# Recurrent-memory attention and MLP: DMA bounces kept apart from DMA transposes, new orders of work, idle matmuls before WO, and W1 in two pieces

## The chip, the cores and the metric

The kernel runs on one core of one Trainium2 chip. The metric is the device time of one execution in microseconds (us); the time before is the median of 12 runs. Engines are called PE (TensorE matmul), PEld (TensorE weight load), DVE (VectorE), ACT (ScalarE), POOL (GpSimd) and SP (SyncE, which here only issues DMAs).

## The reference

The input x has 2048 tokens of 512 values in bfloat16. It is layer-normalised and cut into 64 segments of 32 tokens. An attention layer with 32 heads of 128 runs over the segments one after the other; 8 memory rows, which are the layer's own output of the segment before, stand ahead of each segment:

```python
for s in range(n_seg):                       # 64 segments, strictly one after the other
    h = concatenate([mem, xs])               # 8 memory rows + 32 tokens
    q, k, v = h @ Wq, h @ Wk, h @ Wv         # 512 -> 32 heads x 128
    p = softmax(where(mask, q k^T * scale, -1e9))
    o = (p v) @ Wo                           # 4096 -> 512
    mem = o[:8];  outs.append(o[8:])
h  = x + concatenate(outs)
h2 = h + gelu(layernorm(h) @ w1 + b1) @ w2 + b2    # 512 -> 1792 -> 512
```

## The kernel before

The kernel is recorded as a list of operations by the class Sched and then planned. Each operation has an engine, a duration that the planner believes, and the names that it reads and writes; the waits follow from these names. The planner places the operations of ACT, DVE, POOL and SP by rank (the longest chain behind an operation) plus a table BONUS; an operation recorded with `either` goes to the engine where it would end first. TensorE's order is not planned: it is written by hand in START (segment 0) and ORDER (four lists, one for each segment of a block of four, the position being called sg). BANKS says which PSUM bank a part uses, and BACK which passes run through their four column groups backwards, so that two neighbouring passes can share a loaded weight.

The tokens of a segment are split: 24 of them together with the 8 memory rows form the 32 rows of part A (hT), which depends on the segment before. The other 8 tokens of each of four segments together form the 32 rows of part B (hB), which depends on nothing but x. The parts in ORDER are these:

- Q0, Q1, K0, K1, V0, V1: the passes of part A, each a half of the heads, 16 matmuls of 512 columns on four 32-column tiles (one_pass).
- F0, F1: such passes of part B, for the next block; FB: the output projection of part B for the block before.
- SC0, SC1: scores of the 8 tokens of part B and the memory rows, followed by a softmax on DVE and ACT (sc_mm, sc_softmax); SA: scores of the 24 tokens (sa_mm).
- PV0, PV1, PVA: products with V (pv_c, pv_a); WO: the output projection in eight units (wo, wo_units), of which the 8 memory rows go through a transpose on DVE (TT) and two adds into hT, and so start the next segment.
- TR: DMA transposes. ln1 normalises a block of x and transposes it into hT, from where POOL copies part B's rows into hB. nat transposes a finished block of output (opT) into xT, adds it to x (xr) and stores it (h_mid).

The V of part B is needed in another layout. v_B_spread writes it from VSB to DRAM (v_last, four DMAs) and reads it back into VBD (four DMAs); the text calls this a bounce. On SP all DMAs stand in one queue in the planner's order. The loads at the start are chained in the order x, WV, WK, WQ, WO, more x, with at most three big pieces in flight. After the last segment, WK's space receives the MLP's W1 and W2.

The planner believes that any DMA lands 2 us after its issue (`HOP["sp"]`):

```python
    def lat(p, o):
        if p.is_dma:
            return HOP["sp"]
```

TensorE's program has about 44,000 instructions. `far` cuts it at one place in each 256 instructions, puts a compare-and-branch there (L338; it is never taken) and behind it a prefetch hint for the branch that follows (L342), whose other target lies two cuts on. LINE_AT is the place of the first instruction in its 256, LINE_HINT the place from which a cut may be made, LINE_FIRST that of the extra first hint.

Of the kernel before, what the change touches and what calls it, by code (L numbers as in the profile page):

```python
# [21 lines left out]
LINE_N, LINE_AT, LINE_HINT, LINE_FIRST = 256, 192, 168, 128  # L22
HALVES = ("kqP", "KA", "ZCm", "QA", "VS", "nmc", "EC", "rsc", "PC", "PTC", "OTm", "KB", "QTB", "VSB", "QT")
BONUS = {"EC0": -8.13, "KA0": 12.71, "KA1": -29.28, "KB0": 5.95, "KB1": 40, "OTB": -5.75, "OTm0": 4.47, "OTm1": -45.52, "OTx": 8.96,
         "PA": -27.46, "PC0": 14.2, "PC1": -1.38, "PTC0": -32.47, "PTC1": 12.99, "QT0": -6.56, "QT1": 3.35, "QTB0": 10.94, "QTB1": 14.21,
         "TT": -9.53, "VBD": 3.74, "VS0": 4.35, "VS1": -40, "VSB0": -4.69, "VSB1": 40, "ZCb": -40, "ZCm0": 3.61, "ZCm1": -4.02, "ag": 16.27,
         "hB": 0.6, "hd": -12.71, "hx": 2.32, "kqP0": -0.04, "kqP1": -4.86, "kqP2": -15.51, "kqP3": 14.67, "kqP4": -40, "kqP5": -4.52,
         "nma": -0.27, "nmc1": 22.51, "opB": -1.68, "ps": -16.05, "rs": 2.11, "rs2": 1.39, "rsa": -7.92, "rsc0": -9.47, "rsc1": 10.24,
         "sma": 6.14, "st": 4.36, "st2": -40, "vd": -0.77, "xT": -40, "xn": -3.59, "xn4": -40, "xr": -40}
LEAN = 10.341  # L30
# [4 lines left out]
          (("Q0", 0, 3), ("TR", 0, 1), ("Q0", 3, 4), ("K0", 0, 4), ("Q1", 0, 4), ("K1", 0, 4), ("SC0", 0, 1), ("V0", 0, 4), ("V1", 0, 2),  # L35
           ("SC1", 0, 1), ("V1", 2, 4), ("F0", 0, 1), ("PVA", 0, 1), ("PV0", 0, 1), ("F0", 1, 3), ("WO", 0, 3), ("PV1", 0, 1),
           ("F0", 3, 4), ("WO", 3, 8), ("F1", 0, 1), ("SA", 0, 1), ("F1", 1, 4)),
          (("Q0", 0, 2), ("Q1", 0, 1), ("Q0", 2, 3), ("TR", 0, 1), ("Q0", 3, 4), ("K0", 0, 4), ("Q1", 1, 4), ("K1", 0, 4), ("SC0", 0, 1),
           ("V0", 0, 4), ("V1", 0, 2), ("SC1", 0, 1), ("F0", 0, 2), ("V1", 2, 3), ("PVA", 0, 1), ("PV0", 0, 1), ("V1", 3, 4), ("F0", 2, 4),
           ("WO", 0, 2), ("PV1", 0, 1), ("WO", 2, 8), ("SA", 0, 1), ("F1", 0, 4)),  # L40
          (("Q0", 0, 3), ("TR", 0, 1), ("Q0", 3, 4), ("K0", 0, 4), ("Q1", 0, 4), ("K1", 0, 4), ("SC0", 0, 1), ("V0", 0, 4), ("V1", 0, 1),
           ("PVA", 0, 1), ("SC1", 0, 1), ("F0", 0, 1), ("V1", 1, 4), ("PV0", 0, 1), ("F0", 1, 2), ("SA", 0, 1), ("WO", 0, 2),
           ("PV1", 0, 1), ("WO", 2, 8), ("F0", 2, 4), ("F1", 0, 4)),
          (("Q0", 0, 1), ("TR", 0, 1), ("Q0", 1, 2), ("K0", 0, 1), ("Q0", 2, 4), ("K0", 1, 4), ("Q1", 0, 4), ("K1", 0, 4), ("SC0", 0, 1),
           ("V0", 0, 4), ("V1", 0, 2), ("SC1", 0, 1), ("V1", 2, 4), ("FB", 0, 2), ("PV0", 0, 1), ("FB", 2, 4), ("WO", 0, 2), ("PVA", 0, 1),
           ("PV1", 0, 1), ("WO", 2, 8), ("FB", 4, 6), ("SA", 0, 1), ("FB", 6, 8)),
)
BANKS = (
    dict(Q0=4, Q1=4, K0=7, K1=5, V0=6, V1=5, SC0=7, SC1=4, F0=6, F1=5, FB=6, SA=7, WO=4),
    dict(Q0=6, Q1=4, K0=7, K1=5, V0=7, V1=5, SC0=6, SC1=4, F0=6, F1=5, FB=6, SA=7, WO=4),  # L50
    dict(Q0=6, Q1=4, K0=7, K1=5, V0=7, V1=5, SC0=6, SC1=4, F0=6, F1=5, FB=4, SA=7, WO=4),
    dict(Q0=6, Q1=4, K0=7, K1=5, V0=6, V1=5, SC0=7, SC1=4, F0=6, F1=5, FB=6, SA=7, WO=4),
)
BACK = (("Q1", "K0", "V0", "V1", "F0", "F1"), ("K0", "K1", "F1"), ("K0", "V1", "F0"), ("Q1", "K1"))
BANK0 = dict(K0=7, K1=5, Q0=4, Q1=7, V0=4, V1=5, SC0=6, SC1=7, F0=6, F1=4, FB=6, SA=4, WO=5)
START = (("B", "V", 0, (6, 7)), "V0", "V1", ("B", "K", 0, (4, 6)), "K0", "K1", ("B", "K", 1, (4, 6)), ("B", "Q", 0, (5, 6)), "Q0", "Q1", "Z",
         "SC0", "SC1", ("B", "Q", 1, (5, 4)), "PV0", "PV1", "SA", ("B", "V", 1, (6, 7)), "WO")


class Op:  # L60
    __slots__ = ("eng", "fn", "reads", "writes", "idx", "gidx", "deps", "sig", "sigcount", "waits",
                 "name", "is_dma", "dma_sem", "dur", "mode", "rank", "start", "succ", "prev", "ni", "dma_count", "alts", "kind",
                 "held", "loads", "seg")

    def __init__(self, eng, fn, reads, writes, name, dur, mode):
# [9 lines left out]
        self.alts = self.held = None  # L75
        self.loads = [4]
        k = writes[0] if writes else ""
# [3 lines left out]
class Sched:  # L81
# [60 lines left out]
    def dma(self, fn, kb, reads=(), writes=(), after=(), name=None, eng="sp", behind=None):  # L142

        line = self.dmas if eng == "sp" else self.soft
        old = line[-DMA_SEMS] if len(line) >= DMA_SEMS else None
        o = self.op(eng, fn, reads, writes, 0.07 + kb / 390.0 if eng == "sp" else 1.0, 0, name, list(after) + [old])
        o.is_dma = True
        o.prev = behind
        o.dma_count = 16 * (len(line) // DMA_SEMS + 1)
        line.append(o)  # L150
        return o
# [11 lines left out]
    def lat(p, o):  # L163
        if p.is_dma:
            return HOP["sp"]
        if p.eng == "pe" and o.eng == "pe":
            return 0.0
        return HOP[p.eng] + (0.02 if o.eng == "pe" else 0.0)
# [148 lines left out]
    def far(self, nc, e, zero):  # L317

        ops = self.streams["pe"]
        n, lines, cuts, early = 0, -1, [], None  # L320
        for i, o in enumerate(ops):
            line, at = divmod(n - LINE_AT, LINE_N)
            if early is None and line == 0 and at >= LINE_FIRST:
                early = i
                n += 1
            if line > lines and at >= (LINE_HINT if line else 200):
                assert at < 240
                cuts.append(i)
# [962 lines left out]
```

## Time and profile before

| | us |
|---|---|
| median of 12 runs | 847.77 |
| lowest, highest | 840.73, 852.89 |
| profiled execution, device time | 848.49 |
| its span, first to last instruction | 846.8 |
| PE busy / ACT / DVE / POOL | 791.3 / 583.8 / 520.6 / 179.8 |
| DMA xT<-opT, issue to landing, 14 times (lowest, median, highest) | 2.4, 3.9, 4.3 |
| DMA VBD<-v_last on SP, 56 times (median) | 5.5 |

The span has three stretches: the load of the weights until about 61 us, the 64 segments until about 728 us, and the MLP. A line such as "L667" is a line of the kernel before; passes have the line of a helper (L667, or L433 for matmuls that keep the loaded weight), so groups are told apart by their tiles, which are written out<-in. In the list of waits, "PE ... <- DVE hT" says that TensorE was idle until DVE had written hT; "issue" says that it was idle and that no semaphore explains it. A mean matmul duration in these tables includes the time in the array's pipeline, so the step from one group of four matmuls to the next (0.216 us for 512 columns) is shorter than the duration of one (0.38 us).

### The profile page before, as it was taken

The numbers are of one execution on the slowest core, as the hardware profiler recorded it, in microseconds if no ns is written. First come the engines' busy times: TensorE is split into PE (matmuls) and PEld (weight loads), VectorE is DVE, ScalarE is ACT, GpSimd is POOL, SyncE is SP. The second block draws the span as 40 slices with busy tenths as digits, with TensorE's granted clock in tenths as the row PEclk, the third lists the DMA queues.
The fourth block names the chain that finished last, engine by engine and source line by source line (L and its number), as shares of the span: only waits on it lengthen the run. The fifth ranks groups of instructions, "written<-read, shape, count | busy, mean of one in ns | idle before, by whom it ended". The sixth has DMA issues, their size and how long they took to land.

```text
span 846.8 us, 48411 instructions
## 1 busy us (share of the span) xinstructions
PE 791.3 (93%) x22173; PEld 433.1 (51%) x21613; DVE 520.6 (61%) x1637; ACT 583.8 (69%) x1579; POOL 179.8 (21%) x412
## 2 busy tenths in 40 slices
PE   1758999999899999999999899899999998999998
PEld 0234555555555555555555455455555554554443
DVE  3147667777586868686868576567676776632111
ACT  1337787878687878787878677678787877634442
POOL 3214112222121313131212121212121212042200
PEclk9879999999999999999999999999999999999999
DMA  8951002020202020202020202110111111511000
GB/s 337 367 181 36 9 12 41 16 38 21 41 11 42 17 41 17 41 16 42 16 42 20 44 11 34 16 29 17 29 17 29 41 29 17 196 45 50 25 26 25
DMA packets 49224, 44.15 MB, mean 52 GB/s; under 512 B 18164, under 2 KB 44668, under 8 KB 49020
## 3 DMA queue, kind: packets, MB, share of 16 engines
q1 hardware_dynamic: 48124, 40.00, 17.3%
q8 instruction: 173, 2.83, 1.4%
q0 software_dynamic: 896, 1.06, 0.5%
q14 instruction: 31, 0.25, 0.1%
HBM read 28.98 MB, written 8.39 MB: 44 GB/s over the span
## 4 chain that ended last, share of the span: by engine, by line
PE 84%; DMA 5%; ACT 5%; DVE 3%; issue 2%; SPq 0%; POOL 0%
PE ps L667 42%; PE ps L921 18%; PE ps L1181 6%; PE quad L1188 6%; PE ps L433 3%; PE quad L838 3%; DMA WQ<-in_A_Wq_dram 2%; PE ps L808 2%; PE quad L893 2%; PE ps L867 2%; ACT EC L820 1%; DMA WV<-in_A_Wv_dram 1%; ACT kqP L682 1%; ACT kqP L681 1%; DMA WK<-in_A_Wk_dram 1%
## 5 line engine op out<-in xcount | busy, mean ns | idle before, releaser
L921 PE MATMUL ps<-WO,OT 128*32 128x256 bf16 x4224 | 145.4, 279 | 4.3 <-issue 3.0
L667 PE MATMUL ps<-WQ,hT 128*32 128x512 bf16 x1920 | 130.9, 383 | 5.5 <-DVE hT L927 5.3
L667 PE MATMUL ps<-WV,hT 128*32 128x512 bf16 x1984 | 132.7, 382 | 0.1
L682 ACT ACTIVATE kqP<-ps 128x512 bf16<-128x512 f32 x160 | 95.0, 595 | 46.9 <-PE ps L667 43.8
L681 ACT CAST OT<-quad 128x128 bf16<-128x128 f32 (+1 forms) x192 | 85.0, 443 | 55.0 <-PE quad L842 49.2
L667 PE MATMUL ps<-WK,hT 128*32 128x512 bf16 x1736 | 119.0, 379 | 0.0
L921 PEld LDWEIGHTS ps<-WO,OT 128*32 128x32 bf16 x4224 | 100.4, 97 | 32.4 <-ACT OT L681 9.3
L681 ACT CAST kqP<-ps 128x512 bf16<-128x512 f32 x160 | 93.6, 585 | 21.3 <-PE ps L667 19.9
L709 DVE STREAM_TRANSPOSE KALL<-kqP 128x256 uint32<-128x256 uint32 x160 | 69.3, 433 | 51.0 <-ACT kqP L681 50.6
L679 POOL COPY ZC<-QT 128x128 bf16<-128x128 bf16 x127 | 38.0, 299 | 238.3 <-DVE QT L709 238.1
L667 PEld LDWEIGHTS ps<-WQ,hT 128*32 128x32 bf16 x1920 | 47.2, 97 | 72.2 <-issue 19.8
L667 PEld LDWEIGHTS ps<-WK,hT 128*32 128x32 bf16 x1736 | 47.9, 96 | 63.5 <-issue 26.5
L820 ACT ACTIVATE EC<-ps,nmc 128x64 f32<-128x64 f32 x256 | 77.9, 309 | 3.3 <-DVE nmc L816 2.5
L1184 ACT ACTIVATE WQ<-ps,b1t 128x512 bf16<-128x512 f32 x56 | 38.5, 687 | 58.4 <-PE ps L1181 58.0
L681 ACT CAST VS<-ps 128x512 bf16<-128x512 f32 x128 | 75.1, 587 | 2.2 <-PE ps L667 1.5
L709 DVE STREAM_TRANSPOSE QT<-kqP 128x256 uint32<-128x256 uint32 x128 | 55.3, 432 | 29.2 <-ACT kqP L682 27.6
L933 DVE STREAM_TRANSPOSE TT<-ps 128x256 f32<-128x256 f32 x66 | 29.7, 450 | 64.9 <-PE ps L921 63.8
L667 PEld LDWEIGHTS ps<-WV,hT 128*32 128x32 bf16 x1984 | 47.9, 96 | 31.1 <-ACT kqP L681 7.4
L1188 PE MATMUL quad<-WK,WQ 128*128 128x512 bf16 x224 | 54.4, 379 | 0.5 <-DVE xr L974 0.5
L879 ACT ACTIVATE SA<-SA 128x256 f32<-128x256 f32 x64 | 26.7, 417 | 37.6 <-DVE SA L878 33.8
L1232 DVE TENSOR_TENSOR WV<-quad,WV 128x512 bf16<-128x512 f32 x16 | 11.1, 691 | 66.0 <-PE quad L1188 66.0
L820 ACT ACTIVATION_READ_ACCUMULATOR EC<-ps,nmc 128x1 f32 x256 | 50.3, 197 | 0.0
(115 smaller groups left out, 1299.3 us busy)
## 6 DMA issues: line engine op xcount, KB each, us to landing
WV<-in_A_Wv_dram SPq DMA_DIRECT2D x4, 1024.0 KB, 6.0
WK<-in_A_Wk_dram SPq DMA_DIRECT2D x4, 1024.0 KB, 8.0
WQ<-in_A_Wq_dram SPq DMA_DIRECT2D x4, 1024.0 KB, 8.8
WO<-in_A_Wo_dram SPq DMA_DIRECT2D x4, 1024.0 KB
v_last<-VSB SPq DMA_DIRECT2D x56, 64.0 KB, 2.3
VBD<-v_last SPq DMA_DIRECT2D x56, 64.0 KB
WK<-in_B_w_dram SPq DMA_DIRECT2D x2, 1792.0 KB, 10.6
xr<-in_A_x_dram SPq DMA_DIRECT2D x16, 128.0 KB, 3.4
```

The costliest lines, as they stand in the source:

```text
L667: ins = e.matmul(o, l, m, start=start, stop=stop, tile_position=(0, 32 * j), skip_group_check=True)
L679: "pool": (lambda e: e.tensor_copy(out, src), 0.16 + 1.05e-3 * n)}
L681: return {"act": (lambda e: e.copy(out, src), t_act(n, ps_)), "dve": (lambda e: e.tensor_copy(out, src), 0.165 + 1.0e-3 * n * fast)}
L682: return {"act": (lambda e: e.mul(out, src, scale_), t_act(n, ps_)), "dve": (lambda e: e.tensor_scalar(out, src, scale_, None, ALU.mult), ...
L709: S.op("dve", lambda e: e.transpose(dst.bitcast(U32), kqP[:, i, :].bitcast(U32)), reads=[("kqP", i)], writes=[key], dur=0.435)
L820: ins = e.activation(EC[:, r, sl, :], ps[bank][:, 64 * sl:64 * sl + 64], ACTF.Exp, bias=nmc[:, r, sl:sl + 1], accum_out=smc[:, r, sl:sl + 1])
L879: S.op("act", lambda e: e.activation(SA[:], SA[:], ACTF.Exp), reads=["SA"], writes=["SA"], dur=t_act(256, False))
L921: ins = e.matmul(ps[bank][32 * j:32 * j + 32, 0:256], lhs(slot(h)), wo_cols(h, b), start=(k == 0), stop=(k == 15), tile_position=(0, 32 * ...
L933: S.op("dve", lambda e: e.transpose(tt.rearrange("p c q t -> p (c q t)"), ps[bank][:, 0:256]), reads=[("ps", bank)], writes=[("TT", par)], ...
L1181: ins = e.matmul(ps[bank][:, 0:SBT], W1[:, cc, fc * P:(fc + 1) * P], hnT_of(k, cc // 2)[:, cc % 2, :], start=(cc == 0), stop=(cc == DC - 1))
L1184: S.op("act", lambda e: e.activation(gT[:, fc, :], ps[bank][:, 0:SBT], ACTF.Gelu_apprx_tanh, bias=b1t[:, fc:fc + 1], scale=1.0), reads=[(" ...
L1188: S.op("pe", lambda e: e.matmul(quad[:, t, :], gT[:, fc, t * P:(t + 1) * P], W2[:, fc, :], start=(fc == 0), stop=(fc == FC - 1)), reads=[" ...
```

## The change

The change has these parts.

1. A name "turn" is added. Each DMA transpose (in ln1 and in nat) writes it; each bounce DMA reads it. So a transpose is issued only when all bounce DMAs recorded before it and the transpose before it have landed, and a bounce DMA only when the transpose before it has.
2. Each DMA has its own believed landing time (lag): 4.0 us for hT, 3.2 for xT, 3.2 for the bounce's writes, 5.0 for its reads, 2.0 for others.
3. The bounce of block 1 is issued by SP instead of POOL. nat's add into xr is fixed on DVE (before, the planner chose POOL).
4. stir: 12 matmuls into bank 7 that nothing reads, between units 3 and 4 of the first WO.
5. START is reordered: V of block 1 comes ahead of Q, and Q0 between the two halves of block 0's Q. ORDER, BANKS, BACK, BONUS and LEAN have new values. In ORDER K0 now leads a segment, and SA ends it.
6. far makes its first cut and its first hint one line of 256 earlier, and picks each cut among the places from 172 to 228 by the length of the matmuls around it, with a small weight on the later place.
7. W1 is loaded in two pieces, each with its own name; the MLP's W1 groups wait for their own half.

```diff
-LINE_N, LINE_AT, LINE_HINT, LINE_FIRST = 256, 192, 168, 128
+STIR = 12
+LINE_N, LINE_AT, LINE_HINT, LINE_LAST, LINE_FIRST, LINE_Q, LINE_W = 256, 192, 172, 228, 80, 24, 0.005
...
 ORDER = (
-          (("Q0", 0, 3), ("TR", 0, 1), ("Q0", 3, 4), ("K0", 0, 4), ("Q1", 0, 4), ("K1", 0, 4), ("SC0", 0, 1), ("V0", 0, 4), ("V1", 0, 2),
-           ("SC1", 0, 1), ("V1", 2, 4), ("F0", 0, 1), ("PVA", 0, 1), ("PV0", 0, 1), ("F0", 1, 3), ("WO", 0, 3), ("PV1", 0, 1),
-           ("F0", 3, 4), ("WO", 3, 8), ("F1", 0, 1), ("SA", 0, 1), ("F1", 1, 4)),
...
+          (("K0", 0, 4), ("Q0", 0, 4), ("Q1", 0, 4), ("K1", 0, 4), ("SC0", 0, 1), ("V0", 0, 1), ("TR", 0, 1), ("V0", 1, 4), ("V1", 0, 2),
+           ("SC1", 0, 1), ("F0", 0, 2), ("V1", 2, 3), ("PVA", 0, 1), ("PV0", 0, 1), ("V1", 3, 4), ("F0", 2, 4), ("WO", 0, 2),
+           ("PV1", 0, 1), ("WO", 2, 8), ("F1", 0, 4), ("SA", 0, 1)),
...
-START = (("B", "V", 0, (6, 7)), "V0", "V1", ("B", "K", 0, (4, 6)), "K0", "K1", ("B", "K", 1, (4, 6)), ("B", "Q", 0, (5, 6)), "Q0", "Q1", "Z",
-         "SC0", "SC1", ("B", "Q", 1, (5, 4)), "PV0", "PV1", "SA", ("B", "V", 1, (6, 7)), "WO")
+START = (("B", "V", 0, (6, 7)), "V0", "V1", ("B", "K", 0, (4, 6)), "K0", "K1", ("B", "K", 1, (4, 6)), ("B", "V", 1, (7, 5)),
+         ("B", "Q", 0, (4, None)), "Q0", ("B", "Q", 0, (None, 5)), "Q1", "Z", "SC0", "SC1", ("B", "Q", 1, (5, 7)), "PV0", "PV1", "SA", "WO")
...
         if p.is_dma:
-            return HOP["sp"]
+            return p.lag
...
-        n, lines, cuts, early = 0, -1, [], None
+        early, per, m = None, [], 0
+        for o in ops:
+            per += [o.dur / o.ni] * o.ni
+        n, lines, cuts, cand = 0, -2, [], []
         for i, o in enumerate(ops):
             line, at = divmod(n - LINE_AT, LINE_N)
-            if early is None and line == 0 and at >= LINE_FIRST:
+            if early is None and line == -1 and at >= LINE_FIRST:
                 early = i
                 n += 1
-            if line > lines and at >= (LINE_HINT if line else 200):
+                line, at = divmod(n - LINE_AT, LINE_N)
+            if cand and (line > cand[0][0] or at >= LINE_LAST):
+                cuts.append(max(cand, key=lambda c: c[1:])[-1])
+                lines = cand[0][0]
+                cand = []
+                n += 2
+                line, at = divmod(n - LINE_AT, LINE_N)
+            if line > lines and at >= LINE_HINT:
                 assert at < 240
-                cuts.append(i)
-                lines = line
-                n += 2
+                cand.append((line, min(sum(per[max(0, m - LINE_Q):m]), 0.4) + min(sum(per[m:m + LINE_Q]), 0.3) + at * LINE_W, i))
+            m += o.ni
             n += o.ni + (len(o.waits) >= 2)
+        cuts += [c[-1] for c in cand[-1:]]
...
-                      writes=[("hTx", tb % RBLK)] + [("hTm", r0 + k) for k in range(4)])
+                      writes=[("hTx", tb % RBLK)] + [("hTm", r0 + k) for k in range(4)] + ["turn"], lag=4.0)
...
-            eng = "pool" if bk < 2 else "sp"
+            eng = "pool" if bk < 1 else "sp"
...
+        def stir(n, bank):
+
+            def f(e):
+                return [e.matmul(ps[bank][:, :], ident[:], WV[:, 0, 0:512], start=True, stop=True) for k in range(n)][-1]
+            S.op("pe", f, reads=["ident", ("WV", 0, 0)], writes=[("ps", bank)], dur=0.2 * n, mode=MC, ni=2 * n)
...
             for q in range(8):
+                if idle and q == 4:
+                    stir(*idle)
...
-            S.either({"dve": (add, 0.45), "pool": (add, 1.15)}, reads=["xT", ("xr", bk % XR)], writes=[("xr", bk % XR)])
+            S.op("dve", add, reads=["xT", ("xr", bk % XR)], writes=[("xr", bk % XR)], dur=0.43)
...
-        S.dma(lambda e: e.dma_start(W1, w1_d), 1792, writes=["W1"], after=used["WK"])
+        for a_, b_ in ((0, F // 2), (F // 2, F)):
+            S.dma(lambda e, a_=a_, b_=b_: e.dma_start(W1[:, :, a_:b_], w1_d[:, :, a_:b_]), 896, writes=[("W1", a_ > 0)], after=used["WK"])
         S.dma(lambda e: e.dma_start(W2, w2_d), 1792, writes=["W2"], after=used["WK"])
```

The transpose in nat gets `"turn"` and `lag=3.2` in the same way; the bounce's writes get `reads=["turn"] + ...` with `lag=3.2`, its reads the same with `lag=5.0`.

## The prediction

> **What bounds the kernel now.** I read the busy time by stretches first, with cuts at the end of the weight loads (61 us) and at the end of the recurrence (728 us). Columns: stretch, its length, busy time and instructions of each engine, granted TensorE clock, DMA share, GB/s.
>
> ```profile
> 31.00:61.00 30.00, 14.94 (x292) 7.45 (x288) 7.91 (x24) 8.57 (x24) 7.22 (x14) 0.72 0.81 252
> 61.00:728.00 667.00, 648.63 (x20682) 363.97 (x20126) 475.89 (x1537) 514.93 (x1456) 142.63 (x336) 0.99 0.13 27
> ```
>
> From 61 to 728 us TensorE is busy 648.6 of 667 us: the recurrence is bound by TensorE, and only 18.4 us of idle time can be won there. From 31 to 61 us it is idle for half the time, at a clock of 0.72. Next the waits of TensorE (total, times, longest):
>
> ```profile
> PE quad L838 <- issue: 9.9, 4, 5.7
> PE ps L667 <- DMA WQ<-in_A_Wq_dram: 5.8, 3, 2.2
> PE ps L667 <- DVE hT L927: 5.3, 6, 1.4
> PE ps L921 <- issue: 3.0, 1, 3.0
> PE ps L667 <- issue: 2.5, 1, 2.5
> PE ps L1181 <- DMA WK<-in_B_w_dram: 1.3, 1, 1.3
> ```
>
> "issue" is idle time with no semaphore behind it: 15.4 us, the largest item after the prologue. The timeline of TensorE shows where it lies; nearly all is in four stalls: 5.73, 2.45, 3.54 and 3.03 us.
>
> ```profile
> 32.69 0.65 PE L667 MATMUL ps<-WQ,hB 128*32 128x512 bf16 x8 [1.62 <-DMA WQ<-in_A_Wq_dram]
> 35.34 1.04 PE L667 MATMUL ps<-WQ,hB 128*32 128x512 bf16 x8 [2.00 <-DMA WQ<-in_A_Wq_dram]
> 38.59 1.04 PE L667 MATMUL ps<-WQ,hB 128*32 128x512 bf16 x8 [2.20 <-DMA WQ<-in_A_Wq_dram]
> ...
> 53.27 0.19 PE L838 MATMUL quad<-PTC,VS 32*128 32x16 bf16 x1 [5.73 <-issue]
> ...
> 53.69 3.62 PE L667 MATMUL ps<-WV,hB 128*32 128x512 bf16 x32
> 57.06 2.73 PE L921 MATMUL ps<-WO,OT 128*32 128x256 bf16 x64
> 61.22 1.26 PE L667 MATMUL ps<-WQ,hT 128*32 128x512 bf16 x20 [1.43 <-DVE hT L927]
> ```
>
> The first stall ends at one PV matmul amid its group of 16, so no data was missing: the instruction itself was. The 32 WV matmuls after it take 3.62 us where the same pass takes 1.89 us elsewhere. The other three end at 228.05, 484.12 and 532.66 us. I looked at what the DMA queues do shortly before the first of them:
>
> ```profile
> 213.53 2.27 SPq L770 DMA_DIRECT2D VBD<-v_last  x4
> 215.90 1.22 SPq L624 DMA_TRANSPOSE hT<-xn  x1
> 226.41 1.19 SPq L954 DMA_TRANSPOSE xT<-opT  x1
> ```
>
> Four bounce reads are issued, and 0.1 us after them an hT transpose, while the reads take 5.5 us (median) to land. TensorE's prefetch hint (L342) of that moment stands at 215.65 us, and no instruction packet (queue q8) moves from then to 222.39 us. In the other two cases hT transposes at 471.19 and 519.34 us meet hints at 471.28 and 519.50 us, and again the next packet comes 6.7 and 7.6 us after the hint, against at most 4.8 us after any other hint of the recurrence past 56 us. So three hints, the only ones within 0.3 us of an hT transpose with bounce reads in flight, go unserved, and TensorE later runs into the line of code that never came. Two hints within 0.1 us of transposes with no bounce reads in flight (73.02 us), or with the last few packets of them (69.24 us), were served in 3.4 and 2.2 us.
>
> **What the Trainium skill says.** "Runtime: NRT & Kernel Launch", Instruction fetch mechanics: instruction memory is refilled in 16 KiB blocks of 256 instructions by a DMA queue of the sequencer's own. The page agrees: q8 moved 2.83 MB in 173 packets, 16 KB each. "DMA: Bandwidth & Descriptors", Rules for kernel authors: a transpose next to ordinary DMAs "needs nothing". That is about correctness; the three cases above say that it costs time here. "TensorE: Matmul & The Clock Gate", What's actually happening: after about 3.4 us idle the array runs at half rate until it was busy as long. The 3.62 us pass agrees.
>
> **The change part by part**, against the profiled execution: 848.49 us, span 846.8, 0.7 us above the median of twelve runs.
>
> *Start.* V of block 1 (32 matmuls) moves from behind SA to ahead of Q, and Q0 of segment 0 ahead of the second half of the block's Q. Until 30.47 us nothing changes. V then takes 32/4 x 0.216 = 1.73 us, to 32.2, inside the wait for WQ; the second WQ piece (32.69) lets half a block pass and Q0 run to 34.0; the fourth (38.59) lets the rest and Q1 run to about 40. Before, Q0 and Q1 ended at about 42.2 and PV1 began at 47.28, so 5.1 us later; now PV1 begins at about 45, and WO at about 46, if no stall intervenes. The early hint moves from 27.7 us to the masks (behind the second group of matmuls), and each following one stands a line of code earlier, so lines 1 to 3 are asked for before the WO traffic instead of in it: I take the 5.73 us stall as gone. What is late next is WO. The load stream runs at about 345 GB/s until 52 us, and its last 0.79 MB (six pieces of x and b2 behind WO) take 2.3 us of that: WO's last piece lands at about 49.7. WO units 0 to 3 take 0.94 us, to 47; the 12 idle matmuls 12 x 0.216 = 2.6 us, to 49.6, covered by WO's arrival; without that cover they cost 2.6. Units 4 to 7 end at 50.8; transpose 0.45, two halves of 0.20 and hand-overs let segment 1 begin at about 52.6 instead of 61.22. I take **8.4 us** (6 to 9.5), the stall included.
>
> *Bounces and transposes apart.* SP's order per block becomes four writes, four reads, xT transpose, hT transpose, h_mid, x load; before, hT came right behind the reads. Each transpose now waits for the reads, or the transpose before it, to land. On SP h_mid and the x load queue behind the later hT: about 10 us (from 215.90 to just behind 226.41). The hB copy on POOL waits for hT, with POOL busy 21%; hT is needed a block later. So the waits cost nothing: their cover is a block of 42 us. The three losses go: 2.45 + 3.54 + 3.03 = **9.0 us**. The spread of the runs, 840.73 to 852.89, fits some losses more or fewer; the lowest is 7.8 below the profiled one. New coincidences can't be excluded: 0 to 9 us back, I take 1. The bounce of block 1 moves from POOL to SP: eight issues of 0.52 to 0.69 us leave POOL, and on SP eight of 0.5 to 0.6 us stand behind WO's four, ahead of which nothing waits; the x loads behind four of them start some 2.4 us later, and x of block 2 may land near 53 us, just as DVE wants it (0 to 1 us, inside the start's range).
>
> *xr add from POOL to DVE.* 14 adds of 1159 ns leave POOL for about 0.42 us each on DVE (L974's row). In the built order each stands right behind PTC, and QTB's transpose, statistics and TT stand behind it. POOL waited 77.9 us for xT unharmed; DVE now waits if xT (2.4, median 3.9, at most 4.3 us from issue) comes after the 3.2 us planned. Bounds 0 and 14 x 0.7 = 9.8 us; most is filler work, I take 1.
>
> *W1 in two pieces.* SP issues W1a, W2, W1b. W1 landed 7.94 us after issue, so half of it in about 4, ahead of TensorE's 734.98: the **1.25 us** wait goes. W1b now lands last, near 728.6 + 13.5 = 742; its first reader is the eighth W1 group, at about 748. If that cover went, it would cost what it is late.
>
> *Order, banks, branches, planner.* In the built programs changes between 32-row, 32-column and full matmul groups go from 301 to 303, at about 0.12 us each: nothing. Kept weights go from 560 to 756 matmuls; in this trace four kept ones take 0.22 us like four others: nothing. K0 comes first and Q0 is followed by Q1 and K1 only. From Q0's end to the first score matmul lie ACT 0.595 + DVE 0.432 + POOL 0.299 + about 0.43 of hand-overs (read around 221 us) = 1.76 us, and the cover is 2 x 0.864 = 1.73: even, 0 to 0.4 us a segment. Gains from the other idle time: at most 18.4 - 9.0 us, I take none.
>
> Sum: -8.4 - 9.0 + 1 + 1 - 1.25 = -16.7, so 831.8; less the 0.7 by which the profiled run lies above the median, **831 us**. This is the likeliest case (chance 0.62), its own range 825 to 837.
>
> **Rivals.** *The code fetch finds new coincidences* (0.2): the branches are re-placed by a rule that prefers slow stretches, and two or three of some 170 hints meet a transfer again. Start and W1 remain: 848.5 - 9.7 = 839, 836 to 842. For it: the hints are many; against it: lone transposes harmed none. *The separation never mattered and only luck moves* (0.08): the losses stay as they were and the start is held by a WO that lands late behind the bounces; 848 - 4 = 844 to 847. *Slower: the Q0 chain* (0.1). The score matmuls stand in TensorE's fixed order, so if one DVE instruction of 0.43 us (PTA's transpose) runs ahead of QT's in each segment, 60 x 0.43 = 26 us outweigh the gain: 848.5 - 16.7 + 26 = 858. It decides against the change from 16.7/60 = 0.28 us a segment. Against it: before, score matmuls waited for POOL only twice, 1.2 us in all, and POOL is now emptier.
>
> **Numbers.** 0.5%, about 4 us, is what a measurement tells from no change. Range 824 to 844: it leaves out the slow case and about half of the third. Faster 0.85, same 0.06, slower 0.09.
>
> **What would show it.** Right: segment 1 begins near 53 us; no "issue" stall over 2 us past 60 us; four-segment blocks of 42 us as before; no wait on W1. Wrong: score matmuls waiting for ZC or QT in every segment, "issue" stalls of 2.5 to 3.5 us again, DVE idle behind xT with TensorE idle after it.

## The result, and the profile after

The kernel after takes **832.42 us** (median of 10 runs, 826.18 to 834.49). The kernel before, run beside it, took 848.15 us (median of 41 runs, 836.1 to 860.25). The ratio is **0.985, with a 95% interval of 0.9818 to 0.9882**. Here and below, ratios and their intervals leave out runs more than 1.5% above the fastest run of their kernel, while medians and ranges count every run. The profiled execution of after took 833.81 us (span 832.1). The forecast of 831 us was close, but this was partly luck: two large errors in it cancelled, as this table of the two traces shows. "Predicted" is the sum of the prediction's own terms for that stretch.

| stretch of the span | before, us | after, us | difference | predicted |
|---|---|---|---|---|
| up to the first pass of segment 1 | 61.22 | 54.06 | -7.2 | -8.4 |
| from there to the first W1 group of the MLP | 675.0 | 658.5 | -16.6 | -8.25 |
| first W1 group to first W2 group | 14.35 | 22.45 | +8.1 | 0 |
| the rest of the MLP | 96.2 | 97.1 | +0.9 | 0 |
| span | 846.8 | 832.1 | -14.7 | -16.65 |

Line numbers of after are some 13 to 22 higher than those of before: the passes are L680, the products with PTC L851, WO L943, the W1 groups L1203, the adds behind TT L949.

First the busy time by stretches of after; the columns are those of the prediction's first fence (stretch, length, PE, PEld, DVE, ACT, POOL with instruction counts, granted clock, DMA share, GB/s). The cuts are at the new ends: 53 us and 711 us, and one more around the start of the MLP.

```profile
31.00:53.00 22.00, 15.04 (x316) 7.00 (x307) 7.29 (x21) 9.13 (x27) 4.78 (x9) 0.92 1.08 338
53.00:711.00 658.00, 646.44 (x20900) 368.67 (x20144) 486.63 (x1563) 506.26 (x1470) 125.00 (x319) 1.00 0.12 29
711.00:736.00 25.00, 19.10 (x353) 11.19 (x342) 12.19 (x34) 8.59 (x12) 1.57 (x4) 0.86 0.40 139
```

The clock at the end of the load is 0.92 where it was 0.72. TensorE is idle for 11.6 us of the recurrence, where it was 18.4. The last line is the new weak spot: six idle microseconds and a clock of 0.86 while W1 and W2 load (139 GB/s).

The waits of TensorE in after (total, times, longest):

```profile
PE ps L680 <- DVE hT L949: 6.2, 5, 2.9
PE quad L906 <- issue: 4.9, 1, 4.9
PE ps L680 <- DMA WQ<-in_A_Wq_dram: 2.3, 1, 2.3
PE ps L943 <- DMA WO<-in_A_Wo_dram: 2.1, 2, 1.9
PE ps L821 <- POOL ZC L692: 1.3, 3, 0.5
```

"issue" has fallen from 15.4 us to one stall of 4.9, and no wait on W1 is left. All fourteen traces of this document, those of the experiments among them, show what "issue" is: they have 29 such stalls of over 0.7 us, and 28 of them end 2.3 to 3.0 us after an instruction packet of queue q8 began to move. So these stalls are waits for code (fetch stalls). TensorE's timeline of after shows where the items lie:

```profile
46.38 1.06 PE L943 MATMUL ps<-WO,OT 128*32 128x256 bf16 x32 [0.21 <-DMA WO<-in_A_Wo_dram]
47.37 2.76 PE L927 MATMUL ps<-WV,ident 128*128 128x512 bf16 x12
52.02 1.06 PE L943 MATMUL ps<-WO,OT 128*32 128x256 bf16 x32 [1.89 <-DMA WO<-in_A_Wo_dram]
54.06 0.83 PE L680 MATMUL ps<-WK,hT 128*32 128x512 bf16 x12 [0.97 <-DVE hT L949]
...
678.97 1.00 PE L680 MATMUL ps<-WK,hT 128*32 128x512 bf16 x12 [2.92 <-DVE hT L949]
...
722.05 0.27 PE L906 MATMUL quad<-PTA,VS 32*128 32x24 bf16 x13 [4.88 <-issue]
722.25 1.03 PE L1203 MATMUL ps<-QTB,WK 128*128 128x512 bf16 x2
...
729.49 0.61 PE L1203 MATMUL ps<-QTB,WK 128*128 128x512 bf16 x2
```

At the start the fetch stall is gone, the idle matmuls end by 50.1 us, and TensorE waits 1.89 us more for the second half of WO. At 678.97 us, at the start of the last block's second segment, stands a wait of 2.92 us that the kernel before did not have. At 722.05 us stands a new fetch stall, which ends amid a group of 32 like the stalls of before, and the W1 groups behind it take 1.03 us instead of 0.61 for 4 to 5 us.

SP's queue in after, in the same block as in the prediction, has the transposes in the predicted order behind the reads:

```profile
206.02 2.26 SPq L783 DMA_DIRECT2D VBD<-v_last  x4
220.17 1.48 SPq L976 DMA_TRANSPOSE xT<-opT  x1
222.76 2.48 SPq L637 DMA_TRANSPOSE hT<-xn  x1
```

### The profile page after: what moved, and what is told of

Read it like the earlier page. It is cut to its first block, busy times and chain, and to the rows that moved or that the text cites. A ratio compares the mean times of both kernels' runs of the same rounds, so it can differ in the third digit from the quotient of the medians.

```text
span 832.1 us, 48283 instructions
## 1 busy us (share of the span) xinstructions
PE 785.4 (94%) x22185; PEld 434.6 (52%) x21429; DVE 527.4 (63%) x1651; ACT 571.1 (69%) x1579; POOL 159.4 (19%) x390
## 4 chain that ended last, share of the span: by engine, by line
PE 87%; DMA 6%; DVE 3%; ACT 2%; issue 1%; POOL 0%; SPq 0%
PE ps L680 42%; PE ps L943 18%; PE ps L1203 6%; PE quad L1210 6%; PE ps L446 5%; PE quad L851 3%; DMA WO<-in_A_Wo_dram 2%; PE ps L821 2%; PE quad L906 2%; PE ps L880 2%; DMA WV<-in_A_Wv_dram 2%; DMA WQ<-in_A_Wq_dram 1%; DMA WK<-in_A_Wk_dram 1%; ACT EC L833 1%; PE quad L855 1%
## 5 line engine op out<-in xcount | busy, mean ns | idle before, releaser
L680 PE MATMUL ps<-WV,hT 128*32 128x512 bf16 x1860 | 144.7, 381 | 0.0
L943 PE MATMUL ps<-WO,OT 128*32 128x256 bf16 x4224 | 139.6, 274 | 3.6 <-DMA WO<-in_A_Wo_dram 2.1
L680 PE MATMUL ps<-WK,hT 128*32 128x512 bf16 x1732 | 116.1, 381 | 6.4 <-DVE hT L949 6.2
L680 PE MATMUL ps<-WQ,hT 128*32 128x512 bf16 x1796 | 121.6, 385 | 0.0
L943 PEld LDWEIGHTS ps<-WO,OT 128*32 128x32 bf16 x4224 | 100.4, 96 | 28.0 <-ACT OT L694 5.0
L895 POOL TENSOR_TENSOR PA<-SA,rsa 128x256 bf16<-128x256 f32 x64 | 39.5, 617 | 351.8 <-DVE rsa L894 351.8
L680 PEld LDWEIGHTS ps<-WQ,hT 128*32 128x32 bf16 x1796 | 48.7, 98 | 71.2 <-issue 30.3
L680 PEld LDWEIGHTS ps<-WK,hT 128*32 128x32 bf16 x1732 | 38.2, 95 | 54.9 <-issue 16.5
L680 PEld LDWEIGHTS ps<-WV,hT 128*32 128x32 bf16 x1860 | 48.4, 96 | 34.2 <-issue 15.5
L821 PEld LDWEIGHTS ps<-KALL,ZC 128*32 128x32 bf16 x2048 | 31.4, 96 | 39.4 <-issue 17.5
```

Source lines behind the costliest of these rows:

```text
L680: ins = e.matmul(o, l, m, start=start, stop=stop, tile_position=(0, 32 * j), skip_group_check=True)
L821: ins = e.matmul(ps[bank][32 * j:32 * j + 32, 64 * sl:64 * sl + 64], ZC[:, par, h, :], rhs, start=False, stop=(i == 3), tile_position=(0, ...
L895: pa = lambda e: e.tensor_tensor(PA[:], SA[:], bc(rsa), ALU.mult)
L943: ins = e.matmul(ps[bank][32 * j:32 * j + 32, 0:256], lhs(slot(h)), wo_cols(h, b), start=(k == 0), stop=(k == 15), tile_position=(0, 32 * ...
```

## The experiments

Each kernel was timed beside the kernel before. The rounds ran on different chips, and the median of the kernel before moved from 848.15 to 852.81 us between them, so a difference of 2 or 3 us between the medians of two kernels settles nothing. "Blocks" are the times from one four-segment block to the next, read from the DVE transposes TT: 41.6 to 42.4 us before (without the three with stalls, 41.94 on average), 41.2 to 41.8 after (41.44), leaving out the first and the last.

### Transposes and bounces apart, alone

Edit of the kernel before:

```diff
-                      writes=[("hTx", tb % RBLK)] + [("hTm", r0 + k) for k in range(4)])
+                      writes=[("hTx", tb % RBLK)] + [("hTm", r0 + k) for k in range(4)] + ["turn"])
...
-                S.dma(..., 64, reads=[("vd", bk, i) for i in range(4)], writes=[("VBD", bk % 2, sg)], eng=eng)
+                S.dma(..., 64, reads=["turn"] + [("vd", bk, i) for i in range(4)], writes=[("VBD", bk % 2, sg)], eng=eng)
...
```

(the bounce's writes and the xT transpose likewise.)

> The kernel before with the name "turn" alone: each DMA transpose waits for the bounce reads recorded before it, landing times believed as before (2 us). SP's order per block becomes reads, xT, hT instead of reads, hT, xT. Theory (a prefetch hint beside an hT transpose with bounce reads in flight goes unserved): past 60 us no TensorE stall named issue over 2 us, the 5.7 us stall near 47 us stays; some 848 - 8 = 840 us, 837 to 843. Rival (the separation does not matter, the stalls are luck of where the branches lie): stalls of 2.5 to 3.5 us remain, 846 to 850 us.

Measured: 854.07 us (850.57 to 856.83, 21 runs), ratio 1.01 (1.0076 to 1.0124): slower. No "issue" stall is left in the recurrence, and the runs lie much closer together than those of before. But a wait appeared that nobody had expected. In the list of waits, and in DVE's timeline:

```profile
PE quad L838 <- DVE PTC L827: 15.2, 13, 1.3
```

```profile
312.40 0.59 DVE L949 TENSOR_TENSOR opT<-TTB 64x128 bf16<-64x128 f32 x2
313.14 0.17 DVE L823 RECIPROCAL rsc<-smc 128x2 f32<-128x2 f32 x1
313.34 0.29 DVE L826 TENSOR_TENSOR PC<-EC,rsc 128x128 bf16<-128x128 f32 x1
313.66 0.50 DVE L827 STREAM_TRANSPOSE PTC<-PC 128x128 bf16<-128x128 bf16 x2
```

The add of part B's output into opT (named opB in the tables) now stands ahead of the softmax steps rsc, PC and PTC for which TensorE is waiting, once in each of 11 blocks. "turn" lengthened the chain behind opB, and so its rank. The change gives opB a bonus of -40 instead of -1.68. The next kernel is the same with that one number:

```diff
-         "nma": -0.27, "nmc1": 22.51, "opB": -1.68, ...
+         "nma": -0.27, "nmc1": 22.51, "opB": -40, ...
```

> The kernel before with the name turn alone, as in e1_before_turn, and one number of the planner's table changed: BONUS opB from -1.68 to -40, its value in the kernel after. Theory: the 6 us that turn alone cost came from the planner, not from the DMAs: turn lengthens the chain behind opB, so the copy of opB went ahead of PTC on DVE, and TensorE waited 1.32 us for PTC in each of 11 blocks (14.5 us). With opB put back these waits go, blocks take 42 us, no issue stall over 2 us between 61 and 728 us: 838 to 842. Rival: the waits come from the transposes really landing later; then they stay, 851 to 856.

Measured: 840.05 us (832.9 to 846.04, 22 runs), ratio 0.9974 (0.9936 to 1.0013). The waits on PTC are down to 0.8 us in all, the blocks are 41.6 to 42.5, and no stall over 1 us lies in the recurrence; 4.07 us remain at the start and 3.43 in the W load. The theory held: the wait came from the planner, and one number takes away 14.0 us. Against the kernel before, the median is 12.8 us lower, but the ratio does not tell the two apart; what separation itself gains is shown by the traces and by the next experiment.

### The change without the separation

```diff
-                      writes=[("hTx", ...)] + [("hTm", r0 + k) ...] + ["turn"], lag=4.0)
+                      writes=[("hTx", ...)] + [("hTm", r0 + k) ...], lag=4.0)
...
```

> The changed kernel without "turn"; all else, the believed landing times too, stays. In SP's built order hT stands right behind the bounce reads again. Theory: one to four stalls of 2.5 to 3.5 us between 60 and 700 us come back, each after a hint within 0.3 us of such an hT transpose and no instruction packet for over 6 us; 835 to 842 us, and a wider spread from run to run. Rival (the order and the placing of the branches keep the fetch safe without it): no stall there, 831 to 833 us.

Measured: 846.77 us (834.6 to 856.0, 22 runs), ratio 0.9967 (0.9925 to 1.0009), with a spread like that of before. The interval lies wholly above that of after; the ratios are 1.2% apart, about 10 us, and the medians 14 us. In its profiled run the recurrence is 13.1 us longer than in after, and the losses are back: 3.15, 0.83 and 3.68 us. The first of them, in SP's queue and in TensorE's timeline:

```profile
122.77 2.26 SPq L783 DMA_DIRECT2D VBD<-v_last  x4
125.14 1.22 SPq L637 DMA_TRANSPOSE hT<-xn  x1
```

```profile
138.38 0.39 PE L680 MATMUL ps<-WK,hB 128*32 128x512 bf16 x2 [3.15 <-issue]
```

The picture is that of before: hT right behind the reads, no instruction packet that starts between 124.49 and 132.41 us, the stall ending 13 us after the transpose. But the hint that was lost stood at 126.00 us, 0.86 us behind the transpose, and the one before the stall of 3.68 us at 381.92 us, 2.30 us behind its transpose (the next packet came 6.99 us later). The window of 0.3 us in the prediction was too narrow. Closeness is not enough either: at 427.56 us transpose and reads stand in the same way, and the hint 0.18 us behind the transpose was served in 2.85 us. The three blocks with stalls took 46.97, 42.47 and 47.12 us against 41.4 to 41.6 of their neighbours, so each of the two large losses cost 2 us beyond the stall. In before it is the same. TensorE's timeline there shows one piece of work behind the stall of 2.45 us and again one block later, without a stall:

```profile
229.67 2.36 PE L921 MATMUL ps<-WO,OT 128*32 128x256 bf16 x40
...
272.59 1.28 PE L921 MATMUL ps<-WO,OT 128*32 128x256 bf16 x40
```

The first of them ran at a granted clock of 0.50 (229.6 to 232 us); behind the stall of 3.03 us the clock was 0.50 too (534.5 to 536.5 us).

The traces of all kernels say the same. The four without "turn" (before, this one, and two that follow, e3_before_far and e4_before_order) have two to four stalls of 0.8 to 3.7 us each in the recurrence, twelve in all. The ten with "turn" have none there. So the separation removes the losses, and it does so with old and new tables and branch places alike. Why a fetch fails beside these transfers, and which of the hints near them fails, stays open.

### The branch places alone

Before with the new `far` and its constants (the diff of the change, part 6).

> The kernel before with the new placing of branches and hints alone (first cut and first hint one line of 256 instructions earlier). Theory: the 5.73 us stall near 47 us goes, and with it the half-rate pass after it (3.62 instead of 1.89 us), so segment 1 begins near 54 instead of 61.2 us; the losses in mid-kernel stay random; 839 to 844 us. Rival (the stall comes from the WO traffic, whatever the hints): segment 1 begins at 60 to 62 us, 845 to 851 us.

Measured: 843.2 us (830.77 to 854.03, 21 runs), ratio 0.9924 (0.9884 to 0.9964). Segment 1 begins at 54.52 us. So the branch places alone bring 6.7 of the 7.2 us at the start. The four kernels with the old branch places begin segment 1 at 60.08 to 61.22 us, all after a fetch stall of 2.5 to 5.7 us near 50 us; none of the ten with the new ones has a stall over 0.7 us there. The new START and the idle matmuls together add nothing that can be told from scatter: the eight kernels that share the start of after begin segment 1 between 53.87 and 55.05 us, and the 54.52 us of this one lies among them. Stalls remain: 1.56 and 2.00 us in the recurrence, 3.88 us in the W load.

### Without the idle matmuls

```diff
-            wo_units(lambda sl: OT[:, par, sl, :], ..., bank, None if s else (STIR, 7))
+            wo_units(lambda sl: OT[:, par, sl, :], ..., bank, None)
```

> The kernel after without the 12 idle matmuls. By the prediction they are covered by WO's arrival; WO's last piece landed at about 52 us, so TensorE would idle some 4.5 us before it, and the last four WO units and the first passes of segment 1 would run at half rate for some 3 us: 1 to 2.5 us lost, segment 1 begins at 54 to 55.5: 833 to 835. Rival: the idle matmuls only delay; 831 to 832 or less.

Measured: 833.09 us (831.39 to 835.28, 6 runs). In the trace WO's second half takes 1.90 us instead of 1.06, the first pass of segment 1 takes 1.47 instead of 0.83, and segment 1 begins at 56.09 us. Part of these 2 us is WO itself, whose wait ended at 53.22 instead of 52.02 us. 56.09 us lies outside the 53.87 to 55.05 us of the eight kernels with the idle matmuls, so the trace agrees with the prediction. The medians are too close to settle it, all the more as this run's stall in the W load was 2.75 us and not 4.88. With the 54.52 us of the old START beside it, the new START alone seems to make TensorE idle longer ahead of WO's second half (3.75 us here, 1.72 us there), and the idle matmuls to make up for that; START by itself was not run.

### The orders and tables

The first kernel is before with ORDER, BANKS, BACK, BANK0, BONUS and LEAN of after, but nothing else.

> The kernel before with the new ORDER, BANKS, BACK, BANK0, BONUS and LEAN, the old START. Profile after: a block of four segments takes about 41.3 us against 42.0 before, without any stall. Theory (the order itself gives this): blocks of 41.3 to 41.5 us between losses, so 13 x 0.6 = 8 us less, 838 to 843 us, start and losses unchanged. Rival (the 0.6 us a block come from the DMA side, transposes out of the way or the add off POOL): blocks of 42.0 us, 846 to 850 us.

Measured: 871.63 us (865.2 to 879.06, 6 runs), ratio 1.027 (1.0182 to 1.0358). This missed by 30 us. Besides fetch stalls its blocks take 42.0 to 42.5 us, with 7.1 us of waits on PTC. Two kernels asked what was missing there. One is after with all landing times at 2.0:

```diff
-                      writes=[...] + ["turn"], lag=4.0)
+                      writes=[...] + ["turn"], lag=2.0)
...
```

> The kernel after with every believed landing time back at 2.0 us; turn, orders and tables stay. Theory: orders and tables were fitted to a plan with the true landing times, so the plan of the small engines changes, waits for DVE show between the passes and the four-segment blocks take 42 us or more instead of 41.2 to 41.5: 838 to 850, with no issue stall in the recurrence over 2 us. Rival (the prediction's step: the planner's times are worth nothing): 831 to 834.

Measured: 834.09 us (829.66 to 835.59, 6 runs), blocks of 41.2 to 42.0. So the landing times are worth some 2 us at most, which these medians don't settle (one new wait of 2.46 us for ZC stands at 70.25 us), and the blocks don't need them; the prediction had nothing. The other is after with the add back on POOL:

```diff
-                S.op("dve", add, reads=["xT", ("xr", bk % XR)], writes=[("xr", bk % XR)], dur=0.43)
+                S.op("pool", add, reads=["xT", ("xr", bk % XR)], writes=[("xr", bk % XR)], dur=1.15)
```

> The kernel after with nat's add into xr put back on POOL (1.15 us each, 14 times); all else stays. Theory: the short blocks (41.3 us against 41.8 before) come from a POOL that no longer does these adds while score matmuls wait for ZC, as the blocks of 42.3 in e4_before_order, which had the new order with the add on POOL, suggest: blocks of 42 us or more, score or WO matmuls step up by 0.3 to 0.8 us a block, 837 to 845. Rival (the prediction's step, which charged 1 us for the move to DVE): 831 to 832, blocks of 41.3.

Measured: **840.27 us** (834.2 to 844.71, 22 runs), 7.9 above after; blocks of 41.9 to 42.6. The theory got the size right and the mechanism wrong: the matmuls don't wait for ZC. Here is its list of waits, and DVE, POOL and TensorE in one of its blocks:

```profile
PE quad L851 <- DVE PTC L840: 7.6, 16, 0.6
```

```profile
313.68 1.39 DVE L949 TENSOR_TENSOR opT<-TT 64x96 bf16<-64x96 f32 x2
313.72 1.24 POOL L979 TENSOR_TENSOR xr<-xr,xT 128x512 bf16<-128x512 bf16 x1
...
315.62 0.31 DVE L840 STREAM_TRANSPOSE PTC<-PC 128x128 bf16<-128x128 bf16 x1
...
315.99 0.26 PE L851 MATMUL quad<-PTC,VS 32*128 32x16 bf16 x16 [0.60 <-DVE PTC L840]
```

The two adds into opT take 0.52 us elsewhere (at 672.50 us of after). Here they take 1.39 us, and end 0.11 us after POOL's add. The same happens at all 14 adds of this kernel, with 0.8 to 1.2 us lost each, and at all 14 of e4_before_order. The Trainium skill states the reason ("SBUF — State Buffer", SBUF: two separate sides): VectorE and GpSimd share a pair of SBUF ports, and an instruction of VectorE with two SBUF inputs and one of GpSimd that reads SBUF shut each other out for their whole duration. The trace agrees. In the kernel before, the same adds on POOL met such an instruction only in passing: 1.1 us were lost over all 14.

The last kernel is after with ORDER, BANKS, BACK, BONUS and LEAN of before, opB at -40.

> The kernel after with the order tables of the kernel before (ORDER, BANKS, BACK, BONUS, LEAN), but BONUS opB at -40; turn, landing times, the add on DVE, the start, the branch places and W1's pieces stay. Theory: the new order is worth about half a us a block (K of part B 0.33 and the output projection of part B 0.19 shorter), some 7 us, less 2 us that it loses in segment 60: blocks of 41.8 to 42.1, no issue stall over 2 us in the recurrence, 836 to 841. Rival (the prediction's step, orders at nothing): 830 to 833, blocks of 41.3; or worse than 842, if the old order has no room on DVE for the add.

Measured: **824.59 us** (822.76 to 826.7, 6 runs), ratio 0.9737 (0.9691 to 0.9782). Both the theory and its rival missed. This is 7.8 us faster than after, and the intervals of the two ratios do not overlap. The new orders are therefore not worth 7 us in this company: they cost 7.8 in the median. The blocks tell where. They take 41.57 us on average, the first and the last left out (41.44 in after), so the new order gains 0.13 a block; but the last block takes 41.60 instead of 45.82 us, and the W1 stretch 18.92 instead of 22.45 us, in spite of a stall of 2.75 us in it. The second of these may be chance, since the stall in this stretch differs from kernel to kernel, as the next part shows.

### The last block and the weight load

DVE's timeline of after ahead of the 2.92 us wait:

```profile
676.14 0.42 DVE L890 TENSOR_REDUCE nma<-ps 128x8 f32<-128x256 f32 x1 [1.65 <-PE ps L880]
676.60 0.42 DVE L891 TENSOR_TENSOR SA<-ps,nma 128x256 f32<-128x256 f32 x1
676.94 0.44 DVE L955 STREAM_TRANSPOSE TT<-ps 128x256 f32<-128x256 f32 x1
```

DVE idles 1.65 us for SA's scores and does two steps of them, while TT, which starts the next segment, could have run: WO, which it reads, ended at 675.8 us. Two more steps of SA's softmax follow before the adds into hT at 678.20 us. F1, which elsewhere stands between WO and SA, is empty in the last block. For the W load, the trace shows hints at 707.28, 710.97 and 715.26 us, but no packet that starts between 708.67 and 715.42 us, while W1b and W2 are in flight. The next packet moves at 719.42 us, and TensorE, which had stopped at 717.17, resumes at 722.05. Which packet answers which hint the trace does not say.

This stall is not new with the change, though. Twelve of the fourteen traces have one or two fetch stalls around the W1 groups, the longest in each 1.5 to 5.9 us; e1_before_turn (3.02 us) and e5_turn_opb (3.43 us), with the old tables, the old branch places and W1 in one piece, are among them. Only before and the last kernel of this part, e10_chain_sa, have none. So the trace of before, by which the prediction was made, was a lucky one in this stretch, and its 14.35 us the shortest of all: elsewhere it takes 15.0 to 22.9 us. The ten runs of after lie in two groups, three at 826.2 to 827.3 us and seven at 831.6 to 834.5; whether this stall is what parts them was not traced.

Three kernels treat these two places. Loads chained, one in flight at a time:

```diff
+        w_ = None
...
-            S.dma(lambda e, a_=a_, b_=b_: e.dma_start(W1[...], ...), 896, writes=[("W1", a_ > 0)], after=used["WK"])
-        S.dma(lambda e: e.dma_start(W2, w2_d), 1792, writes=["W2"], after=used["WK"])
+            w_ = S.dma(lambda e, a_=a_, b_=b_: e.dma_start(W1[...], ...), 896, writes=[("W1", a_ > 0)], after=used["WK"] + [w_])
+        for a_, b_ in ((0, FC // 2), (FC // 2, FC)):
+            w_ = S.dma(..., 896, writes=[("W2", a_ > 0)], after=used["WK"] + [w_])
```

> The kernel after with W1 and W2 each in two pieces, and each piece issued only when the one ahead of it has landed (W2's second half has a name of its own). Theory: the 4.88 us stall at 722 us is a fetch of code that was asked for amid two or three big loads in flight; with one piece in flight the fetch gets through: no issue stall over 2 us past 712 us, no W1 groups at half rate, 826 to 828, with all runs together instead of two groups. Cost that could show: W2's second half lands later, at about 731 us, still ahead of its first reader. Rival: the stall is set by the place of the branch alone; it stays, 831 to 834.

Measured: 829.7 us (827.73 to 832.04, 6 runs), a little above what was expected. The range overlaps that of after, so the gain is read from the trace: the stall is 2.02 us and no W1 group runs at half rate; the stretch takes 17.4 us instead of 22.45. The packet that TensorE waits for still moves late, at 718.30 us, and TensorE stands still from 718.68 to 720.71 us; so chaining made the fetch less late, not early. The edit also costs something ahead of the stretch. In DVE's and TensorE's timelines:

```profile
712.56 0.73 DVE L1061 TENSOR_SCALAR WV<-WQ,agg,rst 128x512 bf16<-128x512 bf16 x2 [3.30 <-DMA WQ<-h_mid]
713.21 0.44 DVE L955 STREAM_TRANSPOSE TT<-ps 128x256 f32<-128x256 f32 x1
713.71 0.61 PE L1203 MATMUL ps<-QTB,WK 128*128 128x512 bf16 x2 [1.43 <-DVE TT L955]
```

A load of h_mid is now issued between the pieces (at 705.19 us; in after behind them, at 709.23), and on DVE its user stands ahead of a TT. DVE idles 3.30 us for this load, TT comes behind it, and the first W1 group waits 1.43 us for TT. W1 in one piece:

```diff
-        for a_, b_ in ((0, F // 2), (F // 2, F)):
-            S.dma(lambda e, a_=a_, b_=b_: e.dma_start(W1[:, :, a_:b_], ...), 896, writes=[("W1", a_ > 0)], after=used["WK"])
+        S.dma(lambda e: e.dma_start(W1, w1_d), 1792, writes=[("W1", False), ("W1", True)], after=used["WK"])
```

> The kernel after with W1 loaded in one piece, before W2. Theory: W1 whole lands 8 us after its issue at about 705 us, so the first W1 group (712.5 us) waits 0.5 to 1.5 us; the fetch stall of the W load (4.88 us at 722 us in the kernel after) stays, since W1 and W2 still share the queues: 832.5 to 834.5. Rival: three loads at once, not two, delay the fetch; with two the stall goes and the time falls to 828 to 830 although W1 comes later.

Measured: 833.95 us (831.32 to 835.87, 6 runs). The first W1 group waits 1.21 us again (W1 landed at 713.12 us, 0.35 us before it starts), and the stall stays at 4.25 us. By the trace the pieces are worth about what the prediction said; the medians, 1.5 us apart, don't settle it. Last, the chained loads with one more dependence in segment 60:

```diff
-            S.op("dve", lambda e: e.tensor_reduce(nma[:], v, ...), [("ps", bank)], ["nma"], dur=0.425)
+            S.op("dve", lambda e: e.tensor_reduce(nma[:], v, ...), [("ps", bank)] + ([("hTm", (s + 1) % RING)] if s == NS - 4 else []), ["nma"], dur=0.425)
```

> The kernel e8_after_w_chained (829.7) with one more dependence: in segment 60 alone SA's maximum (nma) waits for the memory rows of the next segment (hTm), so that DVE does TT first. Theory: the 2.97 us wait of the first K pass of segment 61 falls to about 1, as in the other segments of the last block; the hint ahead of the W1 groups also comes half a us earlier, so the 2.02 us stall shrinks: 826 to 828. Rival: SA's softmax, 1.2 us later, becomes the wait; 829 to 830.

Measured: 827.26 us (823.65 to 829.37, 6 runs), ratio 0.9782 (0.9714 to 0.985), an interval that overlaps that of after. TensorE's timeline of its profiled run (823.65 us, the fastest of the six):

```profile
676.78 0.83 PE L680 MATMUL ps<-WK,hT 128*32 128x512 bf16 x12 [0.74 <-DVE hT L949]
...
715.17 0.37 PE L906 MATMUL quad<-PTA,VS 32*128 32x24 bf16 x32
```

The wait is 0.74 us instead of 2.92, and the 32 products with PTA, which the stall had cut in two, run through. The stretch of the W load takes 15.0 us, close to before, with a wait of 1.23 us for TT ahead of it, as in e8_after_w_chained. The spread of the runs suggests that the fetch still comes late in some; their traces were not taken. The tables of before with the chained loads would be the next version to try; it was not run.

## Why the prediction was right, point by point

- **The start, -8.4 predicted, -7.2 measured.** Segment 1 begins at 54.06 us, close to the sign "near 53". The early hints took the stall away, and the kernel with the branch places alone shows that they bring all of it but scatter. The steps that the prediction worked out for the new START gained nothing that can be seen. The term that was mis-sized is WO: its last piece was taken to land at 49.7 us, and TensorE waited for it until 52.02, past the end of the idle matmuls.
- **Separation, -9.0 predicted, about -14 measured.** The mechanism held: without "turn" the losses return, with it alone they are gone. The sum left out what follows a stall. The blocks of before with the three stalls took 46.24, 47.04 and 46.57 us against 41.94 for their neighbours, 14.0 us in all, of which 9.0 are stalls and 5.0 come behind them, where matmuls run at half rate. The prediction cited the rule of the half rate and used it at the start only. By the 3.4 us that it quotes, the stalls of 2.45 and 3.03 us were too short to bring the half rate about; the measurement decides.
- **"At most 0.3 us from an hT transpose" was too narrow**, as the loss at 0.86 us shows. What the runs support is wider and less sharp: with an hT transpose on top of bounce reads, a code fetch asked for in those microseconds can fail, and mostly does not: before has ten hT transposes right behind reads, and three losses. In the three losses of before and the two large ones of e2_after_no_turn, TensorE stops 0.6 to 1.6 us behind the second cut that follows the lost hint.
- **"The waits cost nothing" was right of the DMAs and not of the planner.** A wait that is added changes ranks. With "turn" alone this cost 14 us, as much as the losses had, until opB's bonus was changed. The prediction costed BONUS at zero as a table of its own; it is part of this edit.
- **The add on DVE, +1 predicted, -8 measured in the new order.** The step weighed 0.42 us of DVE against an idle POOL and gave a gain no room, though it names bounds for a loss. The two engines block each other through SBUF; in the old order the add on POOL hardly met one (1.1 us over all 14), in the new one it met an add of DVE on every occasion. In the old order too, the blocks are shorter with the add on DVE (41.57 us against 42.02 in e5_turn_opb); these two kernels differ in more than the add, so the reason there is not settled.
- **Orders and tables, 0 predicted.** Within the middle blocks that was close: 0.1 us a block. But they brought the 2.92 us wait into the last block, which is 4.2 us longer than with the old tables. The prediction asked where Q0's chain would be bare and found it even; the chain of TT, at a place where a part of ORDER is empty, was not looked at. Not taken apart by any run are BANK0, the bounce of block 1 on SP, and one further line of the change: the planner believes 0.05 us more for a hand-over from VectorE to GpSimd.
- **New coincidences, +1 predicted, about +7.5 measured.** In the two traces they came in one place: 4.88 us of stall and some 2.6 us of half rate while W1 and W2 load. The signs looked for them "past 60 us", and there the sign failed. But most of the other kernels have such a stall there too, so what is new is less the coincidence than its absence from the one trace of before; that part of the error is luck. That rival had been given 839 us, since it did not foresee the shorter blocks.
- **W1 in two pieces, -1.25 predicted:** the wait is gone, and comes back as 1.21 us with W1 whole.
- **Blocks "of 42 us as before" failed, on the good side:** 41.44 against 41.94, 6.5 us over 13 blocks. The new orders account for 0.13 of the 0.50 us; the rest is not settled.

So the recurrence is 16.6 us shorter: 14.0 from the losses, 6.5 from the blocks, 1.35 on the way to W1, less 4.0 in the last block; the first block and the first segments give back the 1.3 that are left. Twice as much was gained there as forecast, and the W load of this trace took the surplus back. The slower rival did not come: score matmuls wait for ZC three times, 1.3 us in all.

## What to carry to other kernels

Price a stall with what follows it: on this kernel a lost fetch of 2.5 to 3.5 us cost 4.3 to 5.1. When a dependence is added in a kernel that a planner orders, read the order of every engine again, since the ranks move with it; and when an operation moves from GpSimd to VectorE, look at what VectorE runs beside it, not only at the idle time of the two. Test a set of tuned tables against the old set at the end, with all other parts in place: here the old set was 7.8 us faster in the median. And one trace is not the kernel: the trace of before had no stall in the W load, where twelve of fourteen had one.

## What the hardware showed that was not expected

An add on POOL stretched an 0.52 us pair of DVE adds to 1.39 us. Code fetches come late not only beside a transpose but beside plain weight loads: TensorE stalled 4.88 us with two big loads in flight, 2.02 us with one. After the packet has begun to move, TensorE still waits 2.3 to 3.0 us for its next instruction. Matmuls ran at half rate behind a stall of only 2.45 us. "Runtime: NRT & Kernel Launch", Instruction fetch mechanics, in the Trainium skill calls the cost of crossing a block of code "mostly hidden"; with other DMAs in flight the runs here show it bare.
